# A fused attention and two-stage expert kernel: one gather moved ahead of most of the list scatters, and two weight splits moved ahead of a branch

## The chip, the cores and the metric

The kernel runs on one core of a Trainium2 chip. The metric is the device time of one execution in microseconds (us). A core has five engines that run their own instruction streams and meet at semaphores: TensorE (PE in the rows, its weight loads PEld), VectorE (DVE), ScalarE (ACT), GpSimd (POOL) and SyncE (SP). A letter q behind an engine's name means its instruction queue. Transfers issued by SP and by POOL run on 16 DMA engines.

## The reference, cut to what matters

Attention with normalised q and k gives `x` of 1792 tokens by 768. A first expert layer assigns every token to one of 8 experts, at most 224 tokens each, in order of the logits; a second expert layer routes each token to the expert with the largest logit of the first layer's output.

```python
x = attn_out.transpose(0, 2, 1, 3).reshape(B * S, H * D)
for idx in order:                      # descending logits, tokens x experts
    ...
    assigned[tok] = e                  # at most cap = N // E = 224 tokens for each expert
...
for e in range(E):
    h = np.maximum(x[assigned == e] @ w1[e], 0.0)    # w1[e]: 768 x 1024
    out[assigned == e] = h @ w2[e]                   # w2[e]: 1024 x 768
...
e_idx = np.argmax(logits2, axis=1)     # second layer: gate weight times relu(x @ w1[e]) @ w2[e]
```

## The kernel before, in words

The program is written with a manual order: each engine runs its instructions as the code emits them, and tile pools add the waits.

After attention the kernel finds the assignment by rounds of counting, then ranks every token inside its expert (`ranks`, tile `rk`). The indices of expert 0's tokens come from one-hot matrices (`slots(0)`), and `gather1(0)` fetches its rows of `x_d` into the tile `xg` by two indirect DMAs on POOL (line 959). A check (`judge`) writes `flag_i`; all engines load it (line 1023) and branch on it (line 1024); with these inputs the branch is not taken. While the check runs, TensorE does dummy matmuls (`stay_warm`).

The expert work runs over units `u`: units 0 to 7 are the experts of the first layer, the later ones tiles of the second. A unit is a row of 16 chunks. Chunks 0 to 7 are the first matrix product (`layer1`, lines 1137 to 1145, into a `ph` tile of PSUM, three buffers) and end in `hh` (ACT) and `hl` (DVE). Chunks 8 to 15 are the second one (`layer2`, lines 1177 to 1179, into `py`) with copies to `yr` on ACT. Each product is made of three passes over high and low parts of the operands, so every loaded weight block `raw` is split: ACT writes the high part (line 815), DVE the low part (line 817), into `w1s` or `w2s`. A weight load on SP (line 803) waits until both halves of the block that last used its buffer are split; there are four buffers.

A table `bg` holds background work by unit and chunk: `at(u, c, f, ...)` has `f` emitted in chunk `c` of unit `u`, behind the chunk's matmuls, and with `late=True` behind the chunk's closing operations. In unit `u`, chunks 10 to 15 turn the rows of the next unit: `x_turn(u + 1, j)` transposes `xg` on TensorE (line 1120, into `pt`), ACT writes the high part `xs` (line 1121), DVE the low part (line 1122). So the gather of the next unit's rows must have landed by chunk 10. For expert 0, `x_turn` stands ahead of the loop.

Expert 1's indices come from one-hot matrices too (`slots_next`, `slots2` in chunk 3 of unit 0). The indices of experts 2 to 7 come through lists in memory: `lists` computes for each token its place (`pos1`, tile `p3i`), `lists_go(a, b)` scatters the 16 columns of tokens to the lists by 16 indirect DMAs on POOL (line 1229), in turn into three lists `l1_d[0..2]`, so that each scatter waits for the landing of the one three before it. `list_load` reads the three lists back (SP, line 1250) and `list_sum` adds them on DVE into `idx` (lines 1254 to 1256). `gather(e)` then is POOL's line 959 again. POOL and SP take their instructions in order.

Of the kernel before, what the change touches and what calls it, by code (L numbers as in the profile page):

```python
# [27 lines left out]
def build(ctx, tc, q, k, v, g_q, g_k, m1_gate, m1_w1, m1_w2, modality, m2_gate, m2_bias, m2_w1, m2_w2,  # L28
          out):
    nc = tc.nc  # L30
# [4 lines left out]
    NCH = N // P  # L35
# [770 lines left out]
    def w_split(u, p, i, eng, hi=True, lo=True, c0=0, c1=None):  # L806

        if p == 0 and i == 0 and u not in W1S:
            W1S[u] = wgt.tile([128, 2, DJ, F], FR, name="w1s")
        if p == 3 and i == 0 and u not in W2S:  # L810
            W2S[u] = wgt.tile([128, 2, FB, HD], FR, name="w2s")
        d, j, width = (W1S[u], 2 * p + i, F) if p < 3 else (W2S[u], 2 * (p - 3) + i, HD)
        c = slice(c0, c1 or width)
        if hi:
            nc.scalar.activation(d[:, 0, j, c], RAW[u, p][:, i, c], AF.Copy)  # L815
        if lo:
            eng.tensor_sub(d[:, 1, j, c], RAW[u, p][:, i, c], d[:, 0, j, c].bitcast(FT))  # L817
# [200 lines left out]
    stay_warm(16)  # L1018
    nc.vector.tensor_reduce(add4, ident.rearrange("p (a c) -> p c a", a=4)[:, :E], axis=AX.X, op=OP.add)
    nc.vector.memset(flag_i[:, 1:3], 0)  # L1020
    for i in range(2):
        w_split(0, i // 2, i % 2, nc.vector, hi=False)
    f1 = nc.values_load(flag_i[0:1, 0:1], min_val=0, max_val=4096)
    with tc.If(f1 > 0):
# [75 lines left out]
    def at(u, c, f, *a, late=False):  # L1100
        bg.setdefault((16 * u + c, late), []).append((f, a))

    def run(w, late=False):
        while bg.get((w, late)):
            f, a = bg[w, late].pop(0)
            f(*a)
# [243 lines left out]
    def route(u):  # L1350

        for h in range(2):
            at(u, 13 + h, y_turn, u, 0, h)
            at(u + 1, h, y_turn, u, 1, h)
        at(u + 1, 2, lambda: L4.__setitem__(u, route_logits(u)))
        at(u + 1, 3, route_sum, u)
        at(u + 1, 4, route_choose, u, late=True)
        at(u + 1, 6, route_place, u)
# [37 lines left out]
    def tile_rest():  # L1396

        v = nc.vector
        pe = [P, E, E]
        return [  # L1400
            lambda: v.tensor_sub(cl, base2, took),
            lambda: v.scalar_tensor_tensor(t64[:, :E], eio[:P].to_broadcast(pe), float(T),
                                           cl[:, :, None].to_broadcast(pe), op0=OP.mult, op1=OP.is_lt),
            lambda: v.tensor_add(st, e1792[:P], took),
            lambda: v.tensor_reduce(nt, t64[:, :E], axis=AX.X, op=OP.add),
            lambda: v.scalar_tensor_tensor(cl, nt, -float(T), cl, op0=OP.mult, op1=OP.add),
            lambda: v.tensor_scalar(ns, cl, -float(T - 128), None, op0=OP.is_le),
            lambda: v.tensor_sub(nt, nt, ns),
        ] + tile_table(0, nt, T) + [
            lambda: v.scalar_tensor_tensor(st, nt, float(T), st, op0=OP.mult, op1=OP.add),  # L1410
        ] + tile_table(3, ns, 128) + [
            lambda: v.tensor_scalar(tj[:, 6, 0:1], tj[:, 2, 0:1], float(NT0), None, op0=OP.is_gt),
            lambda: v.tensor_scalar(tj[:, 6, 1:2], tj[:, 5, 0:1], float(NS0), None, op0=OP.is_gt),
            lambda: v.tensor_max(tj[:, 6, 0:1], tj[:, 6, 0:1], tj[:, 6, 1:2]),
            lambda: v.tensor_copy(ti[:, 6, 0:1], tj[:, 6, 0:1]),
        ]
# [51 lines left out]
    for u in range(US):  # L1468
        if u < E:
            W[u] = (m1_w1[u], m1_w2[u])  # L1470
            at(u, 3 if u == E - 1 else 9, route_bias, u)
        for p in range(3, 7):
            for i in range(2):
                c = 2 * (p - 3) + i
                at(u, c, w_split, u, p, i, nc.vector)
        nx = u + 1
        if u == 0:
            for p in range(4, 7):
                at(0, -1, w_load, 0, p)
            for i in range(4):  # L1480
                at(0, i // 2, slots_next, 4 * i, late=True)
            at(0, 3, slots2, 1, oh1)
            at(0, 0, lists, late=True)
            at(0, 1, lists_go, 0, 8)
            at(0, 6, lists_go, 8, NCH)
            at(1, 0, list_load, late=True)
            at(1, 2, list_sum, late=True)
        if u < E:
            route(u)
        if u in (E - 2, E - 1):  # L1490
            if u == E - 2:
                at(u, 0, tile_consts)
            at(u, 9, tile_pick, u - E + 2, late=True)
        if u == E:
            for i, f in enumerate(tile_rest()):
                at(u, 7 + i // 5, f, late=True)
        if nx == US:
            break

        cv, cw, cs, cg, cx = None, (1, 3, 5), (8, 8, 9, 10, 10, 11), 3, range(10, 16)  # L1500
        if u == 0:
            cg = 4
        elif nx >= E:
            cv = 0
        if cv is not None:
            j = nx - E - NP0 - (NT0 if nx in SHORT else 0)
            at(u, cv, tile_values, nx, slice(j, j + 1))
        for p in range(3):
            at(u, cw[p], w_load, nx, p)
        if cv is not None:  # L1510
            at(u, cw[0], tile_list, nx)
            at(u, cg, tile_gather, nx)
        else:
            at(u, cg, gather, nx)
        at(u, max(7, cw[2]), w_load, nx, 3)
        for p in range(3):
            for i in range(2):
                at(u, cs[2 * p + i], w_split, nx, p, i, nc.vector)
            at(u, min(15, cs[2 * p + 1] + 1), w_load, nx, 4 + p)
        for j in range(DJ):  # L1520
            at(u, cx[j], x_turn, nx, j)

    run(-1)
    for i in range(2, 5):
        w_split(0, i // 2, i % 2, nc.vector, hi=False)
    for j in range(DJ):
        x_turn(0, j)
    w_split(0, 2, 1, nc.vector, hi=False)
# [49 lines left out]
```

## Time and profile before

| | |
|---|---|
| time before, median of 3 runs | 881.21 us (880.02 to 882.47) |
| the profiled execution's own time | 879.86 us |
| its span, from the first to the last instruction | 878.0 us |
| TensorE busy | 794.4 us, 90% of the span |
| VectorE, ScalarE, GpSimd busy | 569.9, 466.1, 139.0 us |
| mean granted clock of TensorE | 0.959 of full speed |

The times are read so: the profiled execution is one run, and 1.86 us of it lie outside its span. TensorE is busy for most of the span, so what matters is where it stands still, and where its granted clock is 0.5 (1.2 GHz) and not 1.0 (2.4 GHz).

### The profile page before, as it was taken

Reading aid. Unit: us, or ns where it says so; the run is one execution under the profiler, and the core shown is the slowest. Engines: PE = TensorE matmul, PEld = TensorE weight load, DVE = VectorE, ACT = ScalarE, POOL = GpSimd, SP = SyncE. Lnnn points to the kernel's source line nnn. Section 1 sums busy time; section 2 is a strip of 40 time slices with the busy share of each in tenths; the row PEclk is TensorE's granted clock in tenths of the full one; section 3 lists DMA queues with packets and bytes.
Section 4 is the critical chain, followed back from the end, with each engine's and each line's share of the span. In section 5 each row is a group of like instructions: output and inputs, shape, how many; then the busy total and the mean of one; then the engine's idle time right before and its main releaser. Section 6 shows DMA issues by size and latency. Waiting matters only on the chain.

```text
span 878.0 us, 14928 instructions
## 1 busy us (share of the span) xinstructions
PE 794.4 (90%) x5630; PEld 653.5 (74%) x5630; DVE 569.9 (65%) x1196; ACT 466.1 (53%) x803; POOL 139.0 (16%) x230
## 2 busy tenths in 40 slices
PE   1599999999945869999999999999999999999994
PEld 1233333333434769999999999999999999999983
DVE  4899899893488742745737457484865665655741
ACT  3667776664370344554645556465464554545641
POOL 4430000000032151302201022030110110110000
PEclk9989999999965889999999999999999999999998
DMA  7449979773170684956667566485775865856720
GB/s 174 105 81 208 207 163 219 177 161 74 49 257 19 179 230 99 292 165 209 221 187 263 168 207 214 159 278 172 242 247 185 288 220 177 286 195 222 246 81 19
DMA packets 113785, 161.22 MB, mean 184 GB/s; under 512 B 59328, under 2 KB 77248, under 8 KB 113696
## 3 DMA queue, kind: packets, MB, share of 16 engines
q1 hardware_dynamic: 108928, 143.07, 56.2%
q0 software_dynamic: 4768, 17.02, 5.6%
q8 instruction: 49, 0.80, 0.4%
q14 instruction: 40, 0.33, 0.1%
HBM read 128.78 MB, written 17.22 MB: 166 GB/s over the span
## 4 chain that ended last, share of the span: by engine, by line
PE 60%; DMA 2%; DVE 2%; ACT 1%; issue 1%; POOL 1%; ACTq 0%; DVEq 0%; POOLq 0%
PE py L1177 10%; PE py L1179 10%; PE py L1178 10%; PE ph L1143 9%; PE ph L1144 9%; PE ph L1145 9%; PE pt L1120 2%; DMA l_d<-tok,p3i 1%; PE pt L1289 1%; DVE w2s L817 1%; DMA xg<-x_d,idx 1%; PE pi L1299 1%; ACT w2s L815 1%; POOL l_d L1229 0%; PE pi L1308 0%
## 5 line engine op out<-in xcount | busy, mean ns | idle before, releaser
L1143 PE MATMUL ph<-xs,w1s 128*128 128x224 f32 (+1 forms) x714 | 201.2, 282 | 0.0
L1144 PE MATMUL ph<-xs,w1s 128*128 128x224 f32 (+1 forms) x714 | 196.7, 276 | 0.0
L1145 PE MATMUL ph<-xs,w1s 128*128 128x224 f32 (+1 forms) x714 | 196.6, 275 | 0.0
L1177 PE MATMUL py<-w2s,hh 128*112 128x384 f32 (+1 forms) x496 | 173.7, 350 | 1.4 <-ACT hh L1163 1.3
L1178 PE MATMUL py<-w2s,hl 128*112 128x384 f32 (+1 forms) x496 | 167.6, 338 | 0.0
L1179 PE MATMUL py<-w2s,hh 128*112 128x384 f32 (+1 forms) x496 | 167.5, 338 | 0.0
L817 DVE TENSOR_TENSOR w2s<-raw,w2s 128x768 fp32r<-128x768 f32 x128 | 122.4, 956 | 66.7 <-ACT w2s L815 66.6
L1143 PEld LDWEIGHTS ph<-xs,w1s 128*128 128x128 f32 x714 | 136.1, 191 | 2.9 <-DVE hl L1164 2.9
L1144 PEld LDWEIGHTS ph<-xs,w1s 128*128 128x128 f32 x714 | 136.2, 191 | 0.0
L1145 PEld LDWEIGHTS ph<-xs,w1s 128*128 128x128 f32 x714 | 136.1, 191 | 0.0
L817 DVE TENSOR_TENSOR w1s<-raw,w1s 128x1024 fp32r<-128x1024 f32 x96 | 113.1, 1219 | 17.8 <-ACT w1s L815 14.9
L1122 DVE TENSOR_TENSOR xs<-pt,xs 128x224 fp32r<-128x224 f32 (+2 forms) x92 | 36.5, 397 | 116.1 <-ACT xs L1121 116.1
L815 ACT ACTIVATE w2s<-raw 128x768 fp32r<-128x768 f32 x128 | 107.3, 838 | 0.0
L1121 ACT ACTIVATE xs<-pt 128x224 fp32r<-128x224 f32 (+2 forms) x92 | 33.4, 362 | 124.8 <-PE pt L1120 98.6
L815 ACT ACTIVATE w1s<-raw 128x1024 fp32r<-128x1024 f32 x96 | 96.5, 1058 | 2.1 <-POOL rr L882 2.1
L1177 PEld LDWEIGHTS py<-w2s,hh 128*112 128x112 f32 (+1 forms) x496 | 90.5, 182 | 2.3 <-ACT hh L1163 2.0
L438 ACT ACTIVATE pp<-sc,gs 128x896 f32<-128x896 f32 x72 | 70.0, 1006 | 41.3 <-PE sc L431 41.1
L1178 PEld LDWEIGHTS py<-w2s,hl 128*112 128x112 f32 (+1 forms) x496 | 90.5, 182 | 0.4
L1179 PEld LDWEIGHTS py<-w2s,hh 128*112 128x112 f32 (+1 forms) x496 | 90.1, 182 | 0.2
L1163 ACT ACTIVATE hh<-ph 128x224 fp32r<-128x224 f32 (+1 forms) x120 | 44.3, 369 | 82.1 <-PE ph L1145 77.9
L453 PE MATMUL av<-pp,vt 128*64 128x448 f32 x288 | 64.3, 554 | 0.0
L1164 DVE SCALAR_TENSOR_TENSOR hl<-ph,hh 128x224 fp32r<-128x224 f32 (+1 forms) x120 | 48.3, 402 | 18.3 <-ACT hh L1163 18.3
(321 smaller groups left out, 1089.2 us busy)
## 6 DMA issues: line engine op xcount, KB each, us to landing
raw<-in_moe_w_dram SPq DMA_DIRECT2D x48, 1024.0 KB, 4.9
raw<-in_moe_w_dram SPq DMA_DIRECT2D x64, 768.0 KB, 5.7
y_d<-yr SPq DMA_DIRECT2D x16, 336.0 KB, 4.1
qt<-in_q_dram SPq DMA_DIRECT2D x11, 448.0 KB, 5.2
kt<-in_k_dram SPq DMA_DIRECT2D x24, 192.0 KB, 3.2
vt<-in_v_dram SPq DMA_DIRECT2D x12, 384.0 KB, 4.6
qTs<-qT SPq DMA_DIRECT2D x20, 224.0 KB, 3.7
x_d<-xr SPq DMA_DIRECT2D x12, 336.0 KB, 3.0
```

The costliest lines, as they stand in the source:

```text
L438: nc.scalar.activation(PP[n][:, 2 * g:2 * g + 2, :] if g < 3 else P7[n], ps[:, :w, :S], AF.Exp, scale=gs[:, 4:5])
L453: nc.tensor.matmul(AV[n][64 * s:64 * s + 64, :S], LV[u][:, 3 * (2 * j + s) + g, :], pp[:, 2 * g + s, :], start=(g == 0), stop=False, skip_ ...
L815: nc.scalar.activation(d[:, 0, j, c], RAW[u, p][:, i, c], AF.Copy)
L817: eng.tensor_sub(d[:, 1, j, c], RAW[u, p][:, i, c], d[:, 0, j, c].bitcast(FT))
L1143: nc.tensor.matmul(ph[:, :n], wh, x[:, 0], start=a, stop=False)
L1144: nc.tensor.matmul(ph[:, :n], wh, x[:, 1], start=False, stop=False)
L1145: nc.tensor.matmul(ph[:, :n], wl, x[:, 0], start=False, stop=z)
L1163: nc.scalar.activation(hh, src, AF.Relu)
L1164: nc.vector.scalar_tensor_tensor(hl, src, 0.0, hh.bitcast(FT), op0=OP.max, op1=OP.subtract)
L1177: nc.tensor.matmul(py, a, wh, start=(f == 0), stop=False)
L1178: nc.tensor.matmul(py, b_, wh, start=False, stop=False)
L1179: nc.tensor.matmul(py, a, wl, start=False, stop=(f == FB - 1))
```

## The change

Two places are edited. Ahead of the branch, four low parts of expert 0's W1 are split on DVE in place of two; behind the join one stands ahead of `x_turn` in place of three, and the last one behind `x_turn` as before. In the table, `lists_go` is emitted in three pieces and not two: three scatters in chunk 1 of unit 0, five in chunk 5, eight in chunk 8 (before: eight in chunk 1, eight in chunk 6). Since `gather(1)` stands in chunk 4, it now comes behind three scatters on POOL and not behind eight. `list_load` and `list_sum` move from chunks 0 and 2 of unit 1 to chunks 1 and 3, and the gather of expert 2 from chunk 3 to chunk 4.

```diff
     nc.vector.memset(flag_i[:, 1:3], 0)
-    for i in range(2):
+    for i in range(4):
         w_split(0, i // 2, i % 2, nc.vector, hi=False)
     f1 = nc.values_load(flag_i[0:1, 0:1], min_val=0, max_val=4096)
...
             at(0, 0, lists, late=True)
-            at(0, 1, lists_go, 0, 8)
-            at(0, 6, lists_go, 8, NCH)
-            at(1, 0, list_load, late=True)
-            at(1, 2, list_sum, late=True)
+            at(0, 1, lists_go, 0, 3)
+            at(0, 5, lists_go, 3, 8)
+            at(0, 8, lists_go, 8, NCH)
+            at(1, 1, list_load, late=True)
+            at(1, 3, list_sum, late=True)
...
-        if u == 0:
+        if u < 2:
             cg = 4
...
     run(-1)
-    for i in range(2, 5):
-        w_split(0, i // 2, i % 2, nc.vector, hi=False)
+    w_split(0, 2, 0, nc.vector, hi=False)
     for j in range(DJ):
         x_turn(0, j)
     w_split(0, 2, 1, nc.vector, hi=False)
```

On POOL, in unit 0 (the scatters write `l_d_64` to `l_d_66`, which are the three lists; `xg` is expert 1's rows), the difference of the two orders is:

```order
 L1229 DMA l_d_65<-tok,p3i 1792x2
 L1229 DMA l_d_66<-tok,p3i 1792x2
-L1229 DMA l_d_64<-tok,p3i 1792x2
-L1229 DMA l_d_65<-tok,p3i 1792x2
-L1229 DMA l_d_66<-tok,p3i 1792x2
-L1229 DMA l_d_64<-tok,p3i 1792x2
-L1229 DMA l_d_65<-tok,p3i 1792x2
-L959 DMA xg<-x_d,idx 112x768 x2
+L959 DMA xg<-x_d,idx 112x768 x2
+L1229 DMA l_d_64<-tok,p3i 1792x2
+L1229 DMA l_d_65<-tok,p3i 1792x2
+L1229 DMA l_d_66<-tok,p3i 1792x2
+L1229 DMA l_d_64<-tok,p3i 1792x2
+L1229 DMA l_d_65<-tok,p3i 1792x2
```

The two gather instructions have moved ahead of five scatters; the eight scatters behind them keep their places.

On DVE, at the branch (line 1024) and behind its join, the two places that differ are:

```order
 L1020 MEMSET flag_i 112x2
-L817 TENSOR_TENSOR w1s<-raw,w1s 128x1024 x2
+L817 TENSOR_TENSOR w1s<-raw,w1s 128x1024 x4
 L1023 TENSOR_LOAD flag_i
 L1024 COMPARE_AND_BRANCH
...
 L1024 UNCONDITIONAL_BRANCH x2
-L817 TENSOR_TENSOR w1s<-raw,w1s 128x1024 x3
+L817 TENSOR_TENSOR w1s<-raw,w1s 128x1024
 L1122 TENSOR_TENSOR xs<-pt,xs 128x224
```

Two of the three low parts that stood between the join and the low parts of expert 0's rows (line 1122) have moved ahead of the flag's load.

On SP, at the turn from unit 0 to unit 1 (line 803 are weight loads, line 1250 the list loads, `y_d` a store of results), the difference is:

```order
 L1190 DMA y_d<-yr 112x768
-L1250 DMA l_4155<-l_d_64 112x12x2
-L1250 DMA l_4155<-l_d_65 112x12x2
-L1250 DMA l_4155<-l_d_66 112x12x2
-L803 DMA raw<-in_moe_w_dram 128x2x1024 x3
+L803 DMA raw<-in_moe_w_dram 128x2x1024
+L1250 DMA l_4185<-l_d_64 112x12x2
+L1250 DMA l_4185<-l_d_65 112x12x2
+L1250 DMA l_4185<-l_d_66 112x12x2
+L803 DMA raw<-in_moe_w_dram 128x2x1024 x2
```

The list loads have moved behind one weight load of unit 2.

## Rows read from the trace of the kernel before

**Rows 1.** Waits of TensorE, 283 us to the end: total us, times, longest.

```profile
PE pt L1120 <- DMA xg<-x_d,idx: 8.7, 3, 5.7
```

**Rows 2.** Timeline of TensorE at unit 0's chunk 10: start us, us, what, idle before.

```profile
317.93 0.34 PE L1179 MATMUL py<-w2s,hh 128*112 128x384 f32 x1
324.02 0.45 PE L1120 MATMUL pt<-ident,xg 112*128 112x112 f32 x1 [5.75 <-DMA xg<-x_d,idx]
...
326.82 0.64 PE L1177 MATMUL py<-w2s,hh 128*112 128x384 f32 x1
```

**Rows 3.** Busy time by stretch: PE, PEld, DVE, ACT, POOL, PEclk, DMA, GB/s.

```profile
288.00:293.79 5.79, 3.41 (x25) 3.08 (x26) 5.58 (x10) 2.33 (x7) 0.00 (x0) 1.00 0.64 217
293.79:297.20 3.41, 3.41 (x18) 3.41 (x18) 3.24 (x10) 1.09 (x2) 0.00 (x0) 0.50 0.50 155
...
326.80:331.30 4.50, 4.50 (x16) 4.22 (x17) 1.62 (x2) 1.30 (x2) 3.20 (x4) 0.50 0.01 1
```

**Rows 4.** Timeline of POOL, 283 to 355 us.

```profile
283.12 1.87 POOL L959 DMA_INDIRECT xg<-x_d,idx  x1 [0.30 <-DVE flag_i L1020]
299.74 0.97 POOL L1229 DMA_INDIRECT l_d<-tok,p3i  x1 [14.76 <-DVE w2s L817]
...
306.93 0.94 POOL L1229 DMA_INDIRECT l_d<-tok,p3i  x1 [3.72 <-DMA l_d<-tok,p3i]
...
316.88 0.96 POOL L959 DMA_INDIRECT xg<-x_d,idx  x1 [0.30 <-issue]
318.15 1.61 POOL L959 DMA_INDIRECT xg<-x_d,idx  x1 [0.30 <-issue]
320.06 0.96 POOL L1229 DMA_INDIRECT l_d<-tok,p3i  x1 [0.30 <-issue]
...
332.17 0.94 POOL L1229 DMA_INDIRECT l_d<-tok,p3i  x1 [0.30 <-issue]
...
352.18 1.21 POOL L959 DMA_INDIRECT xg<-x_d,idx  x1 [17.91 <-DVE l L1309]
```

**Rows 5.** Line 959, 317 to 320 us (expert 1's two gathers).

```profile
DMA to landing us min/median/max: 7.1/7.8/8.5
```

**Rows 6.** Line 959, 352 to 355 us (expert 2's two gathers).

```profile
DMA to landing us min/median/max: 5.8/6.1/6.4
```

**Rows 7.** Tile `p3i`, 332.2 to 333.2 us (the last scatter).

```profile
DMA to landing us min/median/max: 6.3/6.3/6.3
```

**Rows 8.** Timeline of DVE, 284 to 353 us.

```profile
284.08 1.22 DVE L817 TENSOR_TENSOR w1s<-raw,w1s 128x1024 fp32r<-128x1024 f32 x1
288.21 3.49 DVE L817 TENSOR_TENSOR w1s<-raw,w1s 128x1024 fp32r<-128x1024 f32 x3 [2.91 <-DVEq L1024]
291.62 0.38 DVE L1122 TENSOR_TENSOR xs<-pt,xs 128x224 fp32r<-128x224 f32 x1
...
298.65 0.17 DVE L1224 CAST p3i<-p3s 112x16 int32<-112x16 f32 x1
...
303.94 0.15 DVE L950 CAST idx<-pt 112x2 int32<-112x2 f32 x1
...
352.42 0.38 DVE L1164 SCALAR_TENSOR_TENSOR hl<-ph,hh 128x224 fp32r<-128x224 f32 x1
```

**Rows 9.** Timeline of ACT behind the join.

```profile
289.52 0.36 ACT L1121 ACTIVATE xs<-pt 128x224 fp32r<-128x224 f32 x1 [26.20 <-DVE w1s L817]
```

**Rows 10.** Timeline of TensorE behind the join.

```profile
289.12 0.32 PE L1120 MATMUL pt<-ident,xg 112*128 112x112 f32 x1 [0.68 <-DMA xg<-x_d,idx]
...
292.06 1.86 PE L1137 MATMUL ph<-xs,w1s 128*128 128x224 f32 x11 [1.55 <-DVE xs L1122]
```

**Rows 11.** Queue instructions of the branch, line 1024: ns, first and last start us.

```profile
L1024 PEldq EVENT_SEMAPHORE  x2: 51/51/51, 287.7 to 287.9; - x2
```

**Rows 12.** Timeline of SP at the start of unit 1.

```profile
342.53 2.34 SPq L1250 DMA_DIRECT2D l<-l_d  x3
347.95 4.97 SPq L803 DMA_DIRECT2D raw<-in_moe_w_dram  x2
```

**Rows 13.** Line 1250, the three list loads.

```profile
DMA to landing us min/median/max: 2.7/3.0/3.0
```

**Rows 14.** Timeline of TensorE at unit 1's chunk 10.

```profile
365.53 0.36 PE L1120 MATMUL pt<-ident,xg 112*128 112x112 f32 x2
```

## The prediction, made before the changed kernel had run

> **What bounds the kernel now.** The first view to read is the busy time of the page: TensorE works for most of the span, so a gain must come out of its idle time or its clock. The second is the list of TensorE's waits behind the branch [rows 1]: the largest is that of the transposes (line 1120) for gathered rows, 8.7 us in three waits. The timeline shows where nearly all of it lies [rows 2]: in chunk 10 of unit 0. The last matmul of chunk 9 ends at 317.93 + 0.34 = 318.27, the first transpose of expert 1's rows starts at 324.02, and layer 2 goes on at 326.82. The table of stretches gives the second price of that stop [rows 3]: from 326.80 to 331.30 TensorE is busy without a gap, but at a granted clock of 0.50, the lower of its levels, 1.2 GHz.
>
> Why are the rows late? POOL's timeline tells [rows 4]. Its scatters begin at 299.74, the fourth waits until 306.93 (3.72 us) because it writes the list that the first one wrote and the first has to land, and so on; the gather of expert 1 stands behind eight of them and is issued at 316.88 and 318.15. The two take 7.1 and 8.5 us to land [rows 5], the second at 318.15 + 8.5 = 326.65, when TensorE resumes. The indices had been ready at 303.94 + 0.15 = 304.09 [rows 8].
>
> A smaller wait stands behind the join: TensorE idles 1.55 us until DVE has written the first low part of expert 0's rows [rows 10]. DVE was occupied by three low parts of weights, 288.21 for 3.49 us [rows 8]. The stretch from 293.79 to 297.20 is at half clock as well [rows 3].
>
> **The splits ahead of the branch.** In the row of three, each further split adds (3.49 - 1.22) / 2 = 1.14 us [rows 8]. Ahead of the branch the second ends at 284.08 + 1.22 = 285.30; two more end at 285.30 + 2 x 1.14 = 287.58. DVE sat idle there anyway, 2.91 us until the join [rows 8], because TensorE's queue passes the join only at 287.7 to 287.9, behind the dummy matmuls [rows 11]. So the two cost nothing; the cover is 0.3 us, and past it each microsecond would count in full. Behind the join one split remains, 288.21 to 289.43. The next instruction, the first low part of the rows, needs ACT's high part, done at 289.52 + 0.36 = 289.88 [rows 9]. It starts at 289.9 and not at 291.62: **1.7 us** earlier, and the six of them and the matmuls that follow run at the same pace as before.
>
> What the clock makes of it is not known. The stretch at 0.50 holds 3.41 us of matmuls [rows 3], of which half, 1.7 us, would be saved if the clock stayed up. It stayed at 1.00 until 293.79 although TensorE had also waited 0.68 us at 289.12 [rows 3, 10]; it fell after the wait of 1.55 us. With that wait gone the saving lies between 0 and 1.7, and the rows favour neither end, since the short wait stays; I take **0.85 us**.
>
> **The gather behind three scatters.** Everything up to here shifts by 1.7 + 0.85 = 2.55 us, so TensorE comes to chunk 10 at 318.1 - 2.55 = 315.5, and expert 1's indices at 304.09 - 2.55 = 301.5. POOL needs 0.9 us from a tile's end on DVE to its issue (298.65 + 0.17 to 299.74) [rows 4, 8], so the gathers are issued at 302.4 and, 1.27 us on (the distance of 316.88 to 318.15), at 303.7. The three scatters are issued by then, since they depend on `p3i`, which comes 1.7 us sooner at least. With the slowest landing seen, 8.5 us, the second lands at 312.2: 3.3 us before it is wanted. The stop of 326.82 - 318.27 = 8.55 us shrinks to the two transposes, at most 0.36 us long in a case without a wait and overlapped by the next matmul [rows 14]; I take 0.15 for them: **8.4 us**. With the stop, the half clock behind it goes: 4.50 / 2 = **2.25 us** [rows 3].
>
> **What is late next.** The three scatters keep their places, and the gathers sit in the hole of 3.72 us in which POOL waited for the first landing anyway [rows 4]. The rest of the scatters lose the 320.06 - 316.88 = 3.2 us that the gathers took in their midst, and start 1.7 us sooner: the last is issued at 332.17 - 4.9 = 327.3 and with 6.3 us to land [rows 7] is there at 333.6. The upper bound, no gain at all in the chain of landings, is 332.17 + 6.3 = 338.5.
>
> These lists now go through an earlier unit 1. With all terms it starts 13.2 us sooner. The list loads stand on SP behind a weight load, 347.95 - 13.2 = 334.8, and so go out from about 335.1 on; the third is issued 1.4 us later, lands in 3.0 us [rows 12, 13], at 339.5. The sum comes on DVE behind `hl` of chunk 3, 352.42 + 0.38 - 13.2 = 339.6: no wait. If the last scatter lands only at 338.5, the lists are there at 338.6 + 1.4 + 3.0 = 343.0, and DVE stands for 3.4 us with `hl` and the splits of `w2s` queued behind it. TensorE has three `ph` buffers, so it runs on for two to three chunks, some 4 to 6 us at 2 us each (18 matmuls of line 1143 and its like), and loses nothing. Expert 2's second gather follows the lists by 0.6 (sum), 0.8 (POOL's start) and 1.5 us (its second issue): 342.4, or 345.9 in the late case; it lands 6.4 us on as before [rows 6], or 8.5 at most: by 350.9, or in the late case 352.3 to 354.4. TensorE asks for it at 365.53 - 13.2 = 352.3 [rows 14]. I take no wait; the bound is 2.1 us.
>
> **Sum.** 1.7 + 0.85 + 8.4 + 2.25 = 13.2 us. Against the profiled execution's 879.86 us this is 866.7. The median of the runs is 1.35 us above that execution, so the forecast for a median is 881.21 - 13.2 = **868.0 us**.
>
> **Rivals.** First, expert 1's gather still comes late, because at 303 us it meets the weight loads on the DMA engines (the share was 0.64 and 0.50 at 288 to 297 us [rows 3]). It would have to take over 11.8 us against 8.5; a wait of 4 us with the half clock behind it gives 874.3. Against it: the landing of 8.5 us was already seen beside loads and scatters. Chance 0.06.
>
> Second, the wait moves to expert 2: the late case above, 2.1 us and 2.25 us of half clock, gives 868.0 + 4.4 = 872.4. For it: a margin of 1.4 us with the slowest landing. Chance 0.13.
>
> Third, POOL cannot issue while DVE splits. Its second issue for expert 0 took 1.87 us [rows 4] beside DVE's splits, against 0.94 to 0.97 for scatters. If it were held until the run of four ends at 287.58, 2.6 us after its end of 284.99 now, expert 0's rows come 2.6 us later, the first low part starts at 292.5 and not at 291.62, and of the gain 8.4 + 2.25 - 0.9 = 9.8 us remain: 871.4. Against it: the issue ended at 284.99, within the second split, which ran until 285.30 [rows 8]. The Trainium skill ("SBUF — State Buffer", section "Who interferes with whom") speaks for it: a VectorE instruction with two SBUF inputs contends with a GpSimd instruction that reads SBUF, and the later one blocks fully until the first has finished. By that rule the issue can slip in between two splits; the trace agrees with a delay of one split, 0.9 us, and not with one of a whole run. Chance 0.04.
>
> Fourth, the slower side: the lists come so late that DVE stands at the sum. Each microsecond of the last scatter's landing beyond about 339 delays expert 2's gather by as much, from landing to resumption 1.5 + 3.0 + 0.6 + 0.8 + 1.5 + 6.4 = 13.8 us. The gain is used up when TensorE resumes at 352.3 + 13.2 - 2.25 = 363.3, that is with a landing at 349.5, 11 us after that of before; at 353 it would be 884.7. Nothing in the rows makes the scatters later than before. Chance 0.03.
>
> Fifth, the order on POOL is not the cause, and the gather lands when the loads of that stretch are through, wherever it stands: then only the splits' part is left, within 0.3% (2.6 us, about what a measurement of this kernel can tell from no change): 879. Against it, 8.5 us from issue to landing. Chance 0.02.
>
> **Numbers.** The forecast has 0.72; its own range is 866 (full clock, and 1.2 us for the spread of the runs) to 870. Faster by over 0.3% are the forecast and the first three rivals, 0.95; the fifth gives 0.02 for the same and the fourth 0.03 for slower. The range takes in the forecast and the second and third rivals: 865.6 to 873.0.
>
> **What the profile will show.** Right: no idle of TensorE before line 1120 in chunk 10 of unit 0, and full clock there; the two issues of line 959 at 302 to 305 us, behind three of line 1229; line 1122 first at about 289.9. Wrong: idle there until a landing after 315; a wait of line 1120 at unit 1's chunk 10, or of DVE before line 1254; or line 959's issue beside the four splits ending after 285.3.

## The result, and the profile after

The changed kernel takes 873.76 us (median of 6 runs, 869.88 to 875.55), the kernel before beside it 881.55 us (6 runs, 880.02 to 882.47): a ratio of 0.9907, with an interval of 0.9882 to 0.9932. It is faster, by about 7.8 us and not by the 13.2 us forecast, and the time lies 0.76 us above the range. The profiled execution took 873.17 us with a span of 871.4 us. One run of one later kernel (949.18 us, at a mean granted clock of 0.828) fell in a slower state of the chip and is left out of that kernel's ratio.

TensorE's waits come first, from 283 us to the end (engine, line, what it waited for, total us, times, longest):

```profile
PE pi L1332 <- DVE d L1322: 2.6, 1, 2.6
...
PE pt L1120 <- DMA xg<-x_d,idx: 1.0, 1, 1.0
PE pt L1120 <- PEq L1024: 0.4, 1, 0.4
```

The 8.7 us of [rows 1] are down to 1.0 us, and that is the landing of expert 0's rows at 290 us, not chunk 10. A new wait has come: 2.6 us at line 1332, which is the first matmul of `route_place`, table work of unit 1.

The span can be cut at marks that both traces have, all of them starts on TensorE (before, after): the first `x_turn` behind the join, 288.15 and 288.98; unit 1, 340.87 and 328.44; unit 2, 377.65 and 369.57; the last unit, 842.0 and 833.9; the end of the span, 878.0 and 871.4. The stretches between are:

| stretch | before | after | difference, us |
|---|---|---|---|
| up to the first `x_turn` | 288.15 | 288.98 | +0.8 |
| unit 0 | 52.72 | 39.46 | -13.3 |
| unit 1 | 36.78 | 41.13 | +4.4 |
| unit 2 to the last unit's start | 464.3 | 464.3 | 0 |
| last unit and output | 36.0 | 37.5 | +1.5 |

Unit 0 gained what the whole sum said, 13.3 us against 13.2 us; the section on the prediction shows that the agreement to 0.1 us is partly luck. Unit 1 gave back 4.4 us. The table of stretches shows where (engines' busy time and instructions, granted clock, share of the DMA engines, GB/s):

```profile
315.00:326.00 11.00, 11.00 (x71) 10.81 (x70) 5.10 (x8) 5.22 (x10) 4.21 (x4) 1.00 1.01 304
344.83:347.39 2.56, 0.00 (x0) 0.00 (x1) 2.33 (x9) 0.94 (x3) 1.49 (x2) 1.00 0.89 339
348.58:351.99 3.41, 3.41 (x16) 3.34 (x15) 3.17 (x13) 2.03 (x5) 0.96 (x1) 0.50 0.89 265
352.00:369.50 17.50, 17.50 (x109) 17.25 (x109) 9.13 (x13) 8.40 (x16) 3.94 (x8) 1.00 0.77 231
```

From 315 to 326 us, where chunk 10 of unit 0 now lies, TensorE is busy throughout at full clock. In unit 1 it stands for 2.56 us and then runs 3.41 us at half clock, which costs another 1.7 us: 4.3 us of the 4.4 us.

What TensorE stands for is on VectorE. This is its timeline in chunks 3 to 6 of unit 1 (start us, us, what, idle before):

```profile
339.76 0.39 DVE L1164 SCALAR_TENSOR_TENSOR hl<-ph,hh 128x224 fp32r<-128x224 f32 x1
343.56 0.18 DVE L1254 CUSTOM_DVE_ANT_0 l<-l 112x48 uint16<-112x48 uint16 x1 [3.41 <-DMA l<-l_d]
344.58 0.18 DVE L1255 CUSTOM_DVE_ANT_0 idx<-l 112x48 uint16<-112x48 uint16 x1 [0.84 <-DMA l<-l_d]
344.80 0.17 DVE L1256 CAST inf<-idx 112x12 f32<-112x12 int32 x1
344.88 0.96 DVE L817 TENSOR_TENSOR w2s<-raw,w2s 128x768 fp32r<-128x768 f32 x1
345.75 0.38 DVE L1164 SCALAR_TENSOR_TENSOR hl<-ph,hh 128x224 fp32r<-128x224 f32 x1
346.05 0.16 DVE L1317 TENSOR_REDUCE nm<-l 112x2 f32<-112x16 f32 x1
...
347.16 0.17 DVE L1322 TENSOR_TENSOR d<-s,nm 112x16 f16<-112x16 f32 x1
```

And this is TensorE in the same place:

```profile
344.55 0.28 PE L1145 MATMUL ph<-xs,w1s 128*128 128x224 f32 x1
347.39 0.18 PE L1332 MATMUL pi<-d,tri 112*128 112x16 f16 x1 [2.57 <-DVE d L1322]
347.43 0.17 PE L1333 MATMUL pi<-d,ones_h 112*128 112x8 f16 x1
```

The sum of the lists (line 1254) stands where the forecast had it, behind `hl` at 339.76, but the lists come 3.41 and 0.84 us later. Behind the sum are queued a split, the next `hl` and `route_choose` (lines 1317 to 1322). Line 1332 reads what `route_choose` writes, and TensorE, which takes its instructions in order, stands at it from 344.83 to 347.39. The `ph` buffers had run out by then as well: TensorE had finished chunk 6, and of the three buffers, which hold chunks 4 to 6, the first comes free only when `hl` of chunk 4 ends, at 345.75 + 0.38 = 346.13. The buffers alone would have held chunk 7 back by 1.3 us; line 1332 makes it 2.57 us.

POOL's timeline shows how the lists got late:

```profile
298.98 0.97 POOL L1229 DMA_INDIRECT l_d<-tok,p3i  x1 [12.52 <-DVE w2s L817]
...
303.10 0.96 POOL L959 DMA_INDIRECT xg<-x_d,idx  x1 [0.66 <-DVE inf L951]
304.36 0.95 POOL L959 DMA_INDIRECT xg<-x_d,idx  x1 [0.30 <-DVE w2s L817]
306.26 0.96 POOL L1229 DMA_INDIRECT l_d<-tok,p3i  x1 [0.95 <-DMA l_d<-tok,p3i]
307.52 1.67 POOL L1229 DMA_INDIRECT l_d<-tok,p3i  x1 [0.30 <-issue]
309.49 1.69 POOL L1229 DMA_INDIRECT l_d<-tok,p3i  x1 [0.30 <-issue]
316.50 1.48 POOL L1229 DMA_INDIRECT l_d<-tok,p3i  x1 [5.32 <-DMA l_d<-tok,p3i]
...
325.18 0.94 POOL L1229 DMA_INDIRECT l_d<-tok,p3i  x1 [4.68 <-DMA l_d<-tok,p3i]
...
333.57 0.94 POOL L1229 DMA_INDIRECT l_d<-tok,p3i  x1 [1.16 <-DMA l_d<-tok,p3i]
```

The gathers stand behind three scatters and are issued at 303.10 and 304.36, as forecast (302.4 and 303.7). They take longer to land than the 8.5 us allowed [rows 5]. The landing times are, for line 959 from 302 to 312 us:

```profile
DMA to landing us min/median/max: 10.1/10.6/11.1
```

The second is there at 304.36 + 11.1 = 315.5, some 0.9 us ahead of the transposes of chunk 10 at 316.35. The scatters behind the gathers land late as well: that of 306.26 took 10.0 us, and POOL then waited 5.32 us and later 4.68 us. For line 1229 from 297 to 336 us the waits of one scatter for an earlier one come to 12.5 us in five, against 11.1 us in five before, and the longest landing is 10.0 us against 8.2 us. The two gathers did fit into the hole of 3.72 us, of which a wait of 0.95 us is left; the waits behind it come to 11.5 us where they were 7.4 us. The fourth scatter landed in 10.0 to 10.2 us in four profiles that have the gathers ahead of it, and in 5.4 us (before) and 8.0 us (splits alone) where they stand behind; what makes it slower was not separated from the weight loads of that stretch. The last scatter is issued at 333.57, not at 327.3.

On SP (start us, us from the first issue to the end of the last) the list loads come next:

```profile
335.54 0.37 SPq L803 DMA_DIRECT2D raw<-in_moe_w_dram  x1
336.21 6.31 SPq L1250 DMA_DIRECT2D l<-l_d  x3
342.62 0.58 SPq L803 DMA_DIRECT2D raw<-in_moe_w_dram  x1
```

A weight load of 1 MB went out 0.67 us ahead of them. Issuing the three took 6.31 us, where the forecast has the third issued 1.4 us after the first, and they landed in 4.9 to 6.8 us each, against 2.7 to 3.0 us [rows 13]: the last is there at about 344.5, not at 339.5. [rows 12] has the same place before the change. The last scatter, issued at 333.57, had landed after 2.1 us, at 335.7, so in this execution the loads wait for the scatters no longer than for the weight load.

### The profile page after: what moved, and what is told of

Same layout as the page of the kernel before. It is cut to its first block, busy times and chain, and to the rows that moved or that the text cites. A ratio compares the mean times of both kernels' runs of the same rounds, so it can differ in the third digit from the quotient of the medians.

```text
span 871.4 us, 14927 instructions
## 1 busy us (share of the span) xinstructions
PE 794.0 (91%) x5630; PEld 653.5 (75%) x5630; DVE 570.0 (65%) x1196; ACT 465.6 (53%) x803; POOL 141.3 (16%) x230
## 4 chain that ended last, share of the span: by engine, by line
PE 52%; DMA 6%; issue 5%; DVE 1%; POOL 1%; SPq 0%; ACT 0%; POOLq 0%; DVEq 0%
PE py L1177 8%; PE py L1179 8%; PE py L1178 8%; PE ph L1143 8%; PE ph L1144 8%; PE ph L1145 8%; DMA l_d<-tok,p3i 4%; PE pt L1120 2%; DMA out_dram<-yr,lt 1%; PE pt L1289 1%; PE pi L1299 1%; DMA l<-l_d 1%; DMA lt<-l_d 0%; DVE w2s L817 0%; SPq L1250 0%
## 5 line engine op out<-in xcount | busy, mean ns | idle before, releaser
L438 ACT ACTIVATE pp<-sc,gs 128x896 f32<-128x896 f32 x72 | 70.0, 1006 | 41.1 <-PE sc L431 40.8
L431 PE MATMUL sc<-qT,kT 128*128 128x448 f16 x144 | 53.1, 369 | 7.9 <-DVE qT L415 4.9
```

What stands on the lines that cost most here:

```text
L431: nc.tensor.matmul(ps[:, s, :S], kT[:, 7 * j + 3 * s + g, :], rhs[s][z], start=(z == 0), stop=(z == 1))
L438: nc.scalar.activation(PP[n][:, 2 * g:2 * g + 2, :] if g < 3 else P7[n], ps[:, :w, :S], AF.Exp, scale=gs[:, 4:5])
```

## The experiments

Each kernel was timed beside the kernel before on the same chip. Each profile is of one execution, so its columns hold less firmly than the ratios. Two causes could make the lists late: the loads stand behind the weight load on SP, or the chain of scatters on POOL ends late. And there were two ways in which lateness could cost time: at line 1332, by VectorE's order, or at the gather of expert 2. A summary first (profile columns from the one profiled execution, unit 1 and line 1332's wait in us; with a fourth list that line is number 1333):

| run | ratio to before | unit 1 | wait at 1332 | waits of VectorE for the lists |
|---|---|---|---|---|
| changed kernel | 0.9907 (0.9882 to 0.9932) | 41.1 | 2.6 | 3.4 + 0.8 |
| the same again | 0.9917 (0.9892 to 0.9941) | 39.6 | 2.2 | 3.9 |
| list loads first | 0.9876 (0.9853 to 0.9898) | 41.0 | 2.4 | 3.8 + 0.3 |
| list sum later | 0.9855 (0.9834 to 0.9875) | 39.2 | none | 1.7 + 1.0 |
| loads first, sum later | 0.9862 (0.9838 to 0.9886) | 38.9 | none | none |
| four lists | 0.9876 (0.9847 to 0.9904) | 41.4 | 2.8 | 2.3 + 2.0 |
| four lists, loads first | 0.9817 (0.9793 to 0.9842) | 36.8 | none | none |
| the same without the splits | 0.9854 (0.9835 to 0.9873) | 36.8 | none | none |
| splits alone | 0.9954 (0.9939 to 0.9970) | 36.8 | none | none |
| gather alone | 0.9940 (0.9918 to 0.9962) | 44.5 | 4.9 | 5.8 + 0.8 |
| gather ahead of all scatters | 0.9935 (0.9912 to 0.9958) | 45.2 | 5.8 | 6.0 + 0.9 |
| before with four lists | 0.9984 (0.9967 to 1.0001) | 36.8 | none | none |

**List loads first.** The list loads go back ahead of the weight load; all else is the changed kernel.

```diff
-            at(1, 1, list_load, late=True)
+            at(1, 0, list_load, late=True)
```

> The changed kernel with the list loads back in chunk 0 of unit 1, so that on SP they stand ahead of the 1024-wide weight load of unit 2 and not behind it; all else as changed. Theory A (the lists came late because the three list loads queue behind that weight load: it was issued at 335.54 and landed at 342.83, they landed at 343.00 to 344.45): the loads go out when the last scatter has landed, about 335.7, land 3 us after their issue as before the change, near 340; DVE's idle of 3.41 + 0.84 us ahead of line 1254 shrinks below 1 us, TensorE's 2.57 us ahead of line 1332 and the half-clock stretch behind it are gone; about 4.3 us less than the changed kernel, 869.5 us. Rival B (they land late because the DMA engines are busy at 336 to 344 us whatever stands ahead on SP): landing stays at 343 or later, the time at 873 to 874 us.

The median was 871.29 us. In the profile VectorE's wait and that of line 1332 stay (2.4 us), and unit 1 takes 41.0 us:

```profile
334.91 0.94 POOL L1229 DMA_INDIRECT l_d<-tok,p3i  x1 [0.30 <-issue]
...
339.43 1.77 SPq L1250 DMA_DIRECT2D l<-l_d  x3
341.31 6.64 SPq L803 DMA_DIRECT2D raw<-in_moe_w_dram  x3
```

The first row is the last scatter on POOL, the others are SP's queue. The loads no longer stand behind a weight load, and three of them take 1.77 us to issue, but they wait for the last scatter and go out at 339.43. The last scatter landed 4.4 us after its issue, at 339.3, against 335.7 in the changed kernel. So the place on SP is not the only cause. The median lies between what the two theories gave; the intervals of this kernel and of the changed one overlap.

**List sum later.** The sum moves behind chunk 5, so behind `route_choose`, and expert 2's gather behind it.

```diff
-            at(1, 3, list_sum, late=True)
+            at(1, 5, list_sum, late=True)
...
-            at(u, cg, gather, nx)
+            at(u, cg if u != 1 else 5, gather, nx, late=u == 1)
```

> The changed kernel with the sum of the lists and expert 2's gather at the end of chunk 5 of unit 1 (behind the operations that choose unit 0's experts), the list loads where the change put them. If it is DVE's order that cost time (the choice of line 1317 to 1322 queued behind the waiting sum, and TensorE's line 1332 behind that choice): TensorE's 2.57 us ahead of line 1332 are gone, the lists still land at 343 to 345, expert 2's gather is issued at 345 to 347 as in the changed kernel and lands by 353, and the time is about 869.5 us. If instead the sum's lateness costs through expert 2's gather or through the weight splits behind it, a wait of line 1120 in unit 1's chunk 10 takes its place, 2 to 4 us, and the time stays at 872 to 875 us.

The median was 868.89 us. VectorE still waits for the lists, but the wait at line 1332 is gone, and so is the half clock. TensorE's waits instead, in the profile:

```profile
PE pt L1120 <- DMA xg<-x_d,idx: 3.1, 3, 1.8
...
PE pt L1120 <- PEq L1024: 0.4, 1, 0.4
```

Of the 3.1 us, 1.75 us lie at the join, where expert 0's rows landed late in this execution, and 1.32 us in chunk 10 of unit 1 (0.50 and 0.82 us), since expert 2's gather is now issued at 347.31 and 348.64 (345.60 and 347.03 in the changed kernel). Unit 1 takes 39.2 us. This shows how the lateness was paid: through what is queued behind the sum on VectorE. Taken out of that queue, the same lateness costs less.

**Splits alone, and gather alone.** The first is the kernel before with only the splits moved, the second the changed kernel with only the splits put back.

```diff
-    for i in range(2):
+    for i in range(4):
         w_split(0, i // 2, i % 2, nc.vector, hi=False)
...
-    for i in range(2, 5):
-        w_split(0, i // 2, i % 2, nc.vector, hi=False)
+    w_split(0, 2, 0, nc.vector, hi=False)
```

> The kernel before with the two splits moved ahead of the branch, nothing else. By the forecast's terms: the first low part of expert 0's rows starts 1.7 us sooner, and 0 to 0.85 us more if the clock stays up behind it; but the gather of expert 1 stays behind eight scatters, which start 1.7 us sooner as well, so 1.7 to 2.6 us less than before: 879 to 880 us. Rival: the four splits end after the dummy matmuls and hold the join, so nothing is gained: 881 to 882 us.

> The changed kernel without the move of the splits: the gather behind three scatters and the later list loads alone. By the forecast's terms the stop in unit 0's chunk 10 and its half clock are gone (8.4 + 2.25 us), unless expert 1's gather, which took 10 to 11 us to land in the changed kernel, lands after TensorE wants it; the wait of DVE on the lists in unit 1 stays (about 4.3 us back): 875 to 876 us. If the splits are worth nothing, the same as the changed kernel, 873.8 us.

The splits alone gave 877.70 us, a ratio of 0.9954: about 4 us less than before, more than the 1.7 to 2.6 us expected. Unit 0 of the profile is only 1.2 us shorter (51.5 us), so where the rest comes from isn't shown. Its stretches show that the clock stays up where [rows 3] had 0.50, while the stop in chunk 10 keeps its half clock behind it:

```profile
293.00:297.00 4.00, 4.00 (x38) 4.00 (x38) 3.86 (x16) 2.19 (x4) 0.00 (x0) 1.00 0.63 197
323.60:328.00 4.40, 3.79 (x12) 3.37 (x13) 1.62 (x2) 1.30 (x2) 2.19 (x2) 0.50 0.04 8
```

The gather alone gave 877.78 us, a ratio of 0.9940, slower than the 875 to 876 us expected: with the wait of 1.7 us at line 1137 back the clock fell at 292.17 for 3.41 us, and TensorE stood at line 1332 for 4.9 us, since the last scatter landed only at 343.7. The stop in chunk 10 goes with the move of the gather and not with that of the splits: with the splits alone TensorE waits 10.0 us for gathered rows, 8.6 us of it at one transpose there; with the gather alone it waits 1.4 us, all of it at the join.

**Four lists.** A fourth list loosens the chain: each scatter waits for the fourth before it, not the third. It costs a fourth load and one more add.

```diff
-    l1_d = [dpool.tile([N, 2], I32, name=f"l1_d{g}") for g in range(3)]
+    l1_d = [dpool.tile([N, 2], I32, name=f"l1_d{g}") for g in range(4)]
...
-            nc.gpsimd.indirect_dma_start(out=l1_d[c % 3],
+            nc.gpsimd.indirect_dma_start(out=l1_d[c % 4],
...
-        for g in range(3):
+        for g in range(4):
...
+        nc.vector.tensor_add(l3[:, 0, 4:], l3[:, 0, 4:], l3[:, 3, 4:])
```

> The changed kernel with four lists in place of three, so that a scatter waits for the landing of the one four before it; four list loads, still behind the weight load of unit 2, and one more addition. Theory C (the lists are late because the chain of landings got longer: in the changed kernel the fourth to sixth scatter took 9 to 10 us to land behind expert 1's gathers, and the last scatter was issued at 333.6, not at 327.3): the last scatter is issued 3 to 6 us sooner. If that were all, the lists would be there when SP has issued four loads, about 342, and DVE's idle ahead of line 1254 falls from 4.2 to under 2 us and TensorE's ahead of line 1332 under 1 us: about 870.5 us. Theory A (the loads queue behind the weight load): they land at 343 to 346 as before, with no gain however early the scatters are: 873 to 875 us.

The median was 873.49 us and unit 1 took 41.4 us: no gain in the profile, and the ratio's interval overlaps the changed kernel's. The last scatter is issued at 330.81, 2.8 us sooner than in the changed kernel (where the fourth to sixth scatter had taken 10.0, 8.9 and 7.6 us to land), but SP's queue reads as that of the changed kernel:

```profile
335.56 0.37 SPq L803 DMA_DIRECT2D raw<-in_moe_w_dram  x1
336.23 5.92 SPq L1250 DMA_DIRECT2D l<-l_d  x4
```

The loads could have gone sooner, and now it is the weight load ahead of them that holds them: it went out only at 335.56, and issuing the four behind it took 5.92 us.

**Four lists, loads first.** The fourth list, and the list loads ahead of the weight load as in the first experiment.

> Four lists as in the run before this, and the list loads in chunk 0 of unit 1, ahead of the weight load. Theories A and C together (each of the two keeps the lists late by itself, which is why the list loads in front alone did not mend the wait: there the last scatter landed at 339.3): the last scatter lands by 333, the lists by 338, DVE does not wait ahead of line 1254, TensorE not ahead of line 1332, unit 1 takes 36.8 us as in the kernel before, and the time is 4.4 us under the changed kernel's, 869 us; 867 in a profile without the clock's fall in the last unit. If the wait stays although both causes are gone, the DMA engines themselves are the cause.

The median was 867.31 us, a ratio of 0.9817 (0.9793 to 0.9842). It beats both kernels. POOL's last scatter, SP's queue and the sum on VectorE:

```profile
330.07 0.94 POOL L1229 DMA_INDIRECT l_d<-tok,p3i  x1 [0.71 <-DMA l_d<-tok,p3i]
...
330.05 5.13 SPq L1250 DMA_DIRECT2D l<-l_d  x4
...
338.48 0.18 DVE L1254 CUSTOM_DVE_ANT_0 l<-l 112x48 uint16<-112x48 uint16 x1
```

The sum starts without a wait, unit 1 takes 36.8 us as before the change, and TensorE is busy in all of it. So there were two causes, and either of them left in place kept the lists late in the profiles: with one removed unit 1 takes 41.0 or 41.4 us, with both removed 36.8 us. In the ratios one edit may be worth something too: 0.9876 for each against 0.9907 and 0.9917 for the changed kernel, with overlapping intervals; both together lie clear of all these.

**Loads first, sum later.** The two first experiments together, with three lists.

> Three lists; the list loads in chunk 0 of unit 1 and the sum with expert 2's gather at the end of chunk 5, the two earlier edits together. With the sum late alone, TensorE's wait ahead of line 1332 was gone but 2.5 us of unit 1 went to a wait for expert 2's gather, which landed at 354.8. With the loads in front, the lists land 2 to 3 us sooner, the gather lands at about 352.5, and unit 1 loses under 1 us: 867 to 868.5 us. If the gather's landing is not set by the lists, it stays at 868.9.

The median was 871.22 us, above the 867 to 868.5 us expected and not better than the later sum alone (their intervals overlap). Nothing waits for the lists, but the gather stands behind chunk 5 and is issued at 344.61 and 345.93, so TensorE waits 1.6 us for expert 2's rows. Of the 2.5 us that the expectation puts down to this gather in the run with the later sum, 1.3 us were such a wait. The later place that takes the wait off VectorE's queue has a price of its own at the gather.

**Gather ahead of all scatters.** No scatter stands ahead of expert 1's gather.

```diff
-            at(0, 1, lists_go, 0, 3)
-            at(0, 5, lists_go, 3, 8)
+            at(0, 5, lists_go, 0, 8)
```

> The changed kernel with no scatter ahead of expert 1's gather: all of the first eight come in chunk 5. If the three scatters ahead are what makes the gather land after 10 to 11 us (and not in 7.1 to 8.5 as before the change), it lands in 6 to 8 us, by 312. If it is the weight loads of that stretch, it takes 10 to 11 us again, until 315. Either way the chain of scatters begins 7 us later, the last is issued near 338 to 340 and the lists land near 347: DVE's wait ahead of line 1254 grows from 4.2 to about 7 us and TensorE's ahead of line 1332 from 2.6 to 5 us or more, so about 876 to 878 us; if the lists' lateness cost nothing, 873.

The median was 878.28 us, a ratio of 0.9935. The last scatter is issued at 340.04, the list loads go out at 346.66, VectorE stands 6.0 and 0.9 us and TensorE 5.8 us at line 1332. In this execution, one of the two slowest of seven, expert 0's rows came late too (2.3 us), so its first microseconds don't compare. Two things follow. The price in unit 1 grows with the lateness of the lists. And the three scatters ahead of the gather cost nothing that counts, since TensorE waits at chunk 10 neither with them nor without: the gather has to be early, but not first. How long the gather took to land can't be read from this trace, so the question of the three scatters or the weight loads stays open.

**Before with four lists.** The kernel before with the edit of the four lists alone.

> The kernel before with four lists in place of three, nothing else: expert 1's gather still stands behind eight scatters, but these wait for one landing and not two. If the chain of landings is what held the gather, it is issued near 311 to 313 and not at 316.9 and 318.2, lands near 320, TensorE's stop in unit 0's chunk 10 shrinks from 8.4 to 1 to 3 us and the half clock behind it shortens or goes: 5 to 9 us less than before, 874 to 878. If the stop is set by the loads of that stretch and not by POOL's order, it stays: 882 to 883.

The median was 881.40 us, a ratio of 0.9984 (0.9967 to 1.0001). POOL's gathers there, and TensorE's second wait for them:

```profile
314.73 1.35 POOL L959 DMA_INDIRECT xg<-x_d,idx  x1 [0.30 <-issue]
316.38 1.95 POOL L959 DMA_INDIRECT xg<-x_d,idx  x1 [0.31 <-DVE w1s L817]
...
327.86 0.45 PE L1120 MATMUL pt<-ident,xg 112*128 112x112 f32 x1 [3.30 <-DMA xg<-x_d,idx]
```

They are issued about 2 us sooner than in [rows 4], and TensorE still waits 8.5 us for them: the second is used at 327.86, 11.5 us after its issue, where it was 326.69 and 8.5 us. So the issue did not set the landing here. Of the two outcomes expected this is the one given to the loads of that stretch. Together with the changed kernel it says that the gather has to be issued well ahead of that stretch; 2 us are not enough. Which transfers hold it there was not tried.

**The best version without the splits.** Four lists and loads first, with the splits as before.

> Four lists with their loads in front of the weight load, the gather behind three scatters, but without the move of the two splits. By the runs so far the splits are worth 1.7 us in TensorE's wait ahead of line 1137 and another 1.7 us because the clock does not fall behind it: 3.4 us more than with them, 870.7 us, with the clock at 0.50 from about 293 for 3.4 us. If the clock's part is chance, only 1.7 us: 869.0.

The median was 870.49 us, a ratio of 0.9854 against 0.9817 with the splits: the splits are worth some 3.2 us here. In the profiled execution, the slowest of the five (873.71 us), the wait at line 1137 behind the join is 2.3 us, and the clock falls behind it:

```profile
287.00:291.50 4.50, 1.94 (x13) 1.26 (x12) 3.05 (x3) 2.33 (x7) 0.00 (x0) 1.00 0.49 172
291.52:298.34 6.82, 6.04 (x28) 6.04 (x29) 5.86 (x18) 1.09 (x2) 0.00 (x0) 0.50 0.67 214
```

**The changed kernel again.** To see how far one execution stands for the kernel.

> The changed kernel once more, on the same chip and beside the same runs of the kernel before as the two above, for a comparison without a change of chip: by its first result 0.9907 of before, 874 to 875 us where before is 882 to 884; the wait ahead of line 1332 is there again.

The median was 875.24 us, a ratio of 0.9917 (0.9892 to 0.9941), in agreement with 0.9907. Line 1332 stood for 2.2 us, at 348.21, and the clock stayed at 1.00 behind it, so that unit 1 took 39.6 us. Unit 0 took 40.9 us, 1.5 us more than in the first profile. Of the six profiles with a wait at that line, five show the half clock behind it and this one does not: it is a price that most of these executions pay, but not all.

## Why the prediction was wrong

**The splits ahead of the branch: right, a little small.** The four ended at 289.05 (three of them start at 285.56 and take 3.49 us), 0.33 us before VectorE could pass the join; the forecast's cover was 0.3 us. One split stands behind it, and the first low part of the rows starts at 291.04, that is 2.06 us behind the first `x_turn`, where it was 3.47 us before: 1.4 us for the 1.7 us of the sum. The clock, which the sum took at half, 0.85 us, stayed at 1.00, so that its whole 1.7 us was saved. The gain of the pair is near 3.1 us against 2.55 us; the best version without the splits found 3.2 us, the splits alone about 4 us. That the clock stays up was left open in the forecast and is now better known: it fell behind the join in all four profiles without the move, and stayed at 1.00 in eight of the nine with it; the ninth is that of the gather ahead of all scatters, where expert 0's rows came 2.3 us late. The reason given for the cover, TensorE's dummy matmuls, does not hold in every execution: in the best version TensorE passed the join at 286.4 and VectorE only at 288.1, and without the move of the splits at 286.6 and 288.3. VectorE waits there for something else as well; what it is stays open.

**The gather behind three scatters: right.** TensorE goes through chunk 10 without a gap and at full clock, so the stop of 8.4 us and its half clock of 2.25 us are gone. Unit 0 as a whole gained 13.3 us; with 3.1 us for the splits and the clock, 10.2 us are left for these two terms of 10.65 us. One term too small and one too large make the total agree. The margin was wrong: 3.3 us had been counted, 0.9 us were left, because the landing took up to 11.1 us and not 8.5 us at most.

**What is late next: the step that failed.** It erred twice. The first error is the time of the lists, forecast at 339.5 and with a late case of 343.0; they came at 344.5. It took the rest of the scatters to lose 3.2 us by the gathers' removal from their midst; but the scatters now follow the gathers, landed in up to 10.0 us, and the chain of three waited longer, not shorter: its last landing came at 335.7 and not at 333.6, still inside the bound of 338.5. It also counted 1.4 us for issuing three list loads behind a weight load and 3.0 us for a landing; that took 6.31 us and up to 6.8 us, and is the larger part here. Other executions turn it round: with the loads first the last scatter landed at 339.3. Either of the two kept the lists late, as the runs with four lists and with the loads first showed. The second error is the price. The step did weigh VectorE standing for 3.4 us, with "`hl` and the splits of `w2s` queued behind it", and gave it no cost, since TensorE "runs on for two to three chunks" on its `ph` buffers and "loses nothing". TensorE did run on to the end of chunk 6, 4.7 us from the end of `hl` at 340.15, but then the buffers were used up 1.3 us before the next `hl` freed one. And the queue behind the sum also holds `route_choose`, and TensorE's own queue holds `route_place` at line 1332, which waits for it. VectorE stood 3.41 and 0.84 us; 2.57 us of it reached TensorE, and 1.7 us of half clock came on top (not in the second profile of the same kernel). The run with the sum behind `route_choose` showed this: the lists no sooner, the wait at 1332 gone.

**The sum of the time.** From the profiled execution before, 13.3 us less in unit 0, 4.4 us more in unit 1, 0.8 us more ahead of the branch and 1.5 us more in the last unit make the 6.6 us between the spans. The 0.8 us ahead of the branch don't come from the edits: before the first of the four splits starts, TensorE is already 1.5 us later (line 914 at 283.60 against 282.12), and 0.7 us of it are won back in the dummy matmuls. The 1.5 us of the last unit lie at half clock between 853.75 and 857.17 us, in a stretch with no edit; the same piece of the program ran at half clock in the profiles of eight of the kernels' executions, that of the best version among them, and at full clock in five, that of the kernel before among them. What decides it stays open. With unit 1's price alone the forecast would have been 881.21 - 13.2 + 4.4 = 872.4 us, just inside the range, so these two terms helped to put the time past its top. But they are read from one execution each, and the largest term by far is the 4.4 us that the sum put at nothing: without it the measured 873.76 us would be 869.4 us, inside the forecast's own 866 to 870 us.

**The rivals.** Expert 1's gather was nearly late: the first rival asked for more than 11.8 us of landing, and 11.1 us were seen (11.5 us in the run with the later sum). The second gave 872.4 by a wait at expert 2's gather; the price and the unit were nearly those measured, but by another way: no wait stands at that gather, which landed at 349.8 and 352.1 for a chunk 10 at 357.44. The run with the later sum showed the second rival's wait, 1.3 us of it. The third did not come about: POOL's second issue for expert 0 went from 284.59 to 286.45, inside the run of splits that ended at 289.05. The prediction's sign for it, an end after 285.3, did come, because everything ahead of the branch was 1.5 us late; the sign should have been given relative to the splits. In the fourth, VectorE does stand at the sum, which was also a sign of being wrong, and the scatters do end later than before (the last issue at 333.57 against 332.17), which the forecast saw nothing in the rows to make them do; but VectorE stands for 4.3 us in all; even with 6.9 us, in the run with the gather ahead of all scatters, the time stayed below that of before. The fifth is refuted as it stands, since the gather landed at 315.5 us once it was issued at 304.36; but the run of the kernel before with four lists shows that within the old stretch an issue 2 us sooner lands no sooner.

## What to carry to other kernels

When a step on an in-order engine may wait, list everything queued behind it up to the next thing that the bottleneck engine reads in order, small table work too, and not only the buffers of the main stream: the bottleneck stops at the first of them. Count the buffers of the main stream to the microsecond too: here they ran out 1.3 us too soon. When two things make a transfer late, taking away one may move little, so test them together as well as one at a time. A transfer moved ahead of others in a queue can lengthen the landings of those behind it: here a chain that waits for landings lost 4.2 us of waiting more, against the 3.2 us of issue time that the move was to save.

## What the hardware showed that was not expected

While the first scatters land, the DMA engines move little although they count as busy. These are the stretches of the changed kernel around its first three scatters and the gathers, and then of the one with the gather ahead of all scatters:

```profile
304.00:307.00 3.00, 3.00 (x30) 3.00 (x29) 1.94 (x4) 1.82 (x4) 1.74 (x3) 1.00 0.41 37
307.00:308.00 1.00, 1.00 (x12) 1.00 (x11) 0.66 (x2) 0.36 (x1) 0.70 (x2) 1.00 0.86 172
308.00:312.00 4.00, 4.00 (x32) 4.00 (x31) 2.46 (x5) 2.80 (x5) 2.88 (x2) 1.00 1.00 338
```

```profile
304.00:308.00 4.00, 4.00 (x52) 4.00 (x51) 3.42 (x9) 1.37 (x4) 1.46 (x2) 1.00 0.81 262
308.00:312.00 4.00, 4.00 (x38) 4.00 (x38) 2.17 (x4) 1.74 (x3) 3.08 (x4) 1.00 1.04 376
...
315.00:318.00 3.00, 3.00 (x19) 3.00 (x18) 3.00 (x4) 2.85 (x4) 0.51 (x1) 1.00 0.58 73
```

Behind the first three scatters the changed kernel moves 37 GB/s for 3 us, against 338 GB/s right after. With no scatters ahead the same time has 262 GB/s, and the quiet stretch (73 GB/s) comes at 315 to 318 us, behind the scatters of 308.71 to 311.24. The kernel before has it too, behind its own first three scatters (25 GB/s at a busy share of 0.71 from 304 to 306 us), and so have the splits alone (23 GB/s at 1.01 from 302 to 304 us); in neither is a gather under way. The weight loads under way in it hardly move. That the gathers of the changed kernel lose the same time, and that this is part of their 10 to 11 us of landing, is likely but not shown; what holds the engines in that stretch was not tried. The list loads, of 8 bytes a piece, show the other side: behind a 1 MB load issued just ahead, three took 6.31 us to issue, and 4.41 us in the second profile of the same kernel; with no weight load just ahead of them, 2.34 us before the change, 1.77 us with the loads first, but 3.75 us with the loads first and the sum later.
